# Strassen's method for the input product of a second MLP layer, one Trainium2 core

## Chip, core and metric

One NeuronCore of a Trainium2 chip runs the whole program. The metric is device time in microseconds (us) of one execution. Engines are called TensorE (PE, with its weight loads as PEld), VectorE (DVE), ScalarE (ACT), GpSimd (POOL) and SyncE (SP, which issues the DMAs).

## What is computed

Attention with rotary embedding, then two MLP layers (called moe and moe2 in the reference) on the same 1152 tokens, width 512, hidden width 2048. The change concerns the second layer:

```python
x = attention_with_rope(q, k, v)           # B=2, H=8, S=576, D=64 -> (1152, 512)
h = x @ w_in;   g = where(h > 0, h, exp(min(h, 0)) - 1);   x = g @ w_out      # layer 1
h = x @ w2_in;  g = h * tanh(log1p(exp(h)));               out = g @ w2_out   # layer 2
```

The four weight matrices arrive as 64-bit floats, the rest as 32-bit floats.

## The kernel before

**Precision.** Each fp32 operand of a product is held as a rounded half "h" and a remainder "l" (lo), and each product is made of three passes: h·h, h·l, l·h. For activations, `XH`/`XL` hold the layer's input (hidden on partitions in four chunks `cc` of 128, tokens along the row).

**Weights.** A block of weights (512 KB) lands in `raw` (three buffers), is turned from 64-bit to 32-bit in `wu` by one GpSimd multiplication (L96, "rebase") and three VectorE bit operations (L100, L104, L108), is rounded by ScalarE (L126), and GpSimd subtracts to get the lo half (L127). There are 16 input blocks and 16 output blocks per layer. A pair of feature blocks (2 x 128 hidden features) is the unit of the input product.

**Input product.** `g1_mm` (L180) makes one unit: one feature pair times one third of the tokens (384), in 24 matmuls of 384 columns, into a PSUM tile `ps_s`; that tag has two buffers, so a unit waits until the unit two before has been read. A layer has 8 pairs x 3 thirds = 24 units. Layer 1 follows with the ELU on ScalarE and VectorE, layer 2 with Mish on ScalarE (L772), rounding (L773) and a subtraction on VectorE (L774).

**Output product.** Layer 1 (`g2_first`, L783): 24 matmuls of 384 columns per tile of third x two output chunks, added into `Y`, and in the last group `XH` (L803) and `XL` (L804) of the next layer are made from it. Layer 2 (`g2_second`, L806): per group of four feature blocks and per 128 tokens 12 matmuls of 512 columns, added into `Y` by VectorE (L820), 36 tiles of them.

**Order.** In layer 1 every engine runs in the order in which the code is written. In layer 2 ScalarE alone does; for the other engines a scheduler chooses. On every engine an instruction that waits holds up all behind it. Layer 2's first units were placed among layer 1's last output tiles.

Of the kernel before, what the change touches and what calls it, by code (L numbers as in the profile page):

```python
# [18 lines left out]
MANUAL = {mybir.EngineType.Activation}  # L19
# [7 lines left out]
def kernel(  # L27
# [23 lines left out]
    GF = 4  # L51
# [18 lines left out]
    late_pool = [None]  # L70

# [14 lines left out]
    def weight_stages(key):  # L86
        kind, c = key
        raw = raws.pop(key)
        if wide:


            w = raw.rearrange("p (n w) -> p n w", w=2)
            low, high = w[:, :, 0], w[:, :, 1]
            u = wpool.tile([128, 512], F32, tag="wu", name="wu", bufs=2)
            ui = u.bitcast(I32)
            nc.gpsimd.tensor_scalar(  # L96
                out=u, in0=high.bitcast(F32), scalar1=REBASE, scalar2=0.0, op0=ALU.mult, op1=ALU.add
            )
            yield
# [3 lines left out]
            yield  # L103
# [3 lines left out]
            yield  # L107
# [3 lines left out]
            yield  # L111
        else:
            u = raw
        even = c // GF % 2 == 0
        tag, bufs = ("wi", "wo")[kind] + ("0" if even else "1"), GF
        if kind and even:
            bufs = GF // 2
            tag += "b" * (c % GF >= bufs)
        pool = wpool if even and tag[-1] != "b" else late_pool[0]
        hi = pool.tile([128, 512], F32R, tag=tag + "h", name=tag + "h", bufs=bufs)  # L120
        lo = pool.tile([128, 512], F32R, tag=tag + "l", name=tag + "l", bufs=bufs)
# [4 lines left out]
        nc.scalar.activation(out=hi, in_=u, func=AF.Copy)  # L126
        nc.gpsimd.tensor_tensor(out=lo, in0=u, in1=plain(hi), op=ALU.subtract)  # L127

    jobs = []
    for g in range(2 * NG):  # L130
        for kind in range(2):
            jobs += [(kind, g * GF + i) for i in range(GF)]
    loaded, opened, njob = [0], [0], [0]
# [21 lines left out]
    def weight_part(depth=2):  # L155
        while len(running) < depth and opened[0] < len(jobs):
            open_job()
        if running:
            advance(0)

    def weight_job():
        n = min(njob[0] + 1, len(jobs))
        while njob[0] < n:
            weight_part()
# [36 lines left out]
    def tmp(tag):  # L201
        return late_pool[0].tile([128, 2 * CH], F32, tag=tag, name=tag, bufs=4)
# [7 lines left out]
    def galloc(m, fp, t):  # L210
        i = g_count[0] % GB
        g_count[0] += 1
        pool, tag, bufs = (main, "ge", GE) if i < GE else (late_pool[0], "g", GB - GE)
# [552 lines left out]
    units = [(m, g * GF // 2 + k, t) for m in range(2) for g in range(NG) for t in range(NT // CH) for k in range(GF // 2)]  # L766

    def moe(mp, early):
        def mish(unit, o):
            s = tmp("ta")  # L770
            gh, gl = galloc(*unit)
            nc.scalar.activation(out=v2(s), in_=o[:, :, :CH], func=AF.Mish)  # L772
            nc.scalar.activation(out=gh, in_=s, func=AF.Copy)  # L773
            nc.vector.tensor_tensor(out=gl, in0=s, in1=plain(gh), op=ALU.subtract)  # L774

        Yt = []

        def get_y():
            if not Yt:
                Yt.append(mp.tile([128, NC * NT], F32, name="Y"))  # L780
            return Yt[0]

        def g2_first(g, t, ep):  # L783
            o = g_pool[0].tile([128, 2, 512], F32, tag="g", name="ps_g", bufs=2)
            k = 0
            for f in range(g * GF, g * GF + GF):
                for w, i in ((0, 0), (0, 1), (1, 0)):
# [6 lines left out]
                    k += 1  # L794
            pv = o[:, :, :CH]
            part = (slice(None), slice(2 * ep, 2 * ep + 2), slice(t * CH, t * CH + CH))
            y = get_y().rearrange("p (e s) -> p e s", e=NC)[part]
# [4 lines left out]
            if g == NG - 1:  # L802
                nc.scalar.activation(out=XH[part], in_=y, func=AF.Copy)  # L803
                nc.vector.tensor_tensor(out=XL[part], in0=y, in1=plain(XH[part]), op=ALU.subtract)  # L804

        def g2_second(g, t):  # L806
            o = g_pool[0].tile([128, 512], F32, tag="h", name="ps_h", bufs=2)
            c, s0 = divmod(t * 128, CH)
            k = 0
            for f in range(NF + g * GF, NF + g * GF + GF):  # L810
                gh, gl = (g_part(f, c, i)[:, s0:s0 + 128] for i in range(2))
                hi, lo = WO[f]
                for l, w in ((gh, hi), (gl, hi), (gh, lo)):
                    nc.tensor.matmul(o, lhsT=l, rhs=w, start=(k == 0), stop=(k == 3 * GF - 1))  # L814
                    k += 1
            y = get_y().rearrange("p (t e) -> p t e", e=DM)[:, t, :]
            if g == 0:
                nc.scalar.activation(out=y, in_=o, func=AF.Copy)
            else:
                nc.vector.tensor_tensor(out=y, in0=y, in1=o, op=ALU.add)  # L820
                if g == NG - 1:
                    nc.sync.dma_start(out=out[t * 128:t * 128 + 128, :], in_=y)

        half = len(units) // 2
# [3 lines left out]

        def run_g2(it):
            (g2_second if it[0] else g2_first)(*it[1:])  # L830

        def due(n):
            return 2 * GF + (n + 1) * 2 * GF // (UB * NT // CH)

        def count(n):
            if n < half - 1:
                return (0, 0, 2, 1, 2, 2)[n] if n < 6 else 1 + n % 2
            return max(0, min(len(jobs), due(n)) - njob[0])
# [157 lines left out]
```

## Time and profile before

| | |
|---|---|
| runs: median (lowest to highest) of 3 | 555.0 us (554.99 to 555.21) |
| the profiled execution's own time | 555.24 us |
| its span, first to last instruction | 553.4 us |
| TensorE busy | 544.7 us (98%) |
| VectorE, ScalarE, GpSimd busy | 369.1, 266.9, 246.7 us |
| granted TensorE clock | 1.000 of full speed |

The profiled time is 1.9 us more than the span, which is work around the first and last instruction. A share of busy time is a mean over stages: attention up to about 145 us, layer 1 up to about 360 us, layer 2 to the end. A busy TensorE counts pipelined matmuls, so what one matmul costs is read from the spacing of their starts and not from the duration of one.

### The profile page before, as it was taken

The page shows a single profiled execution, that of the slowest core. Times are in us where ns is not written, and L with a number is a line of the kernel's source. Part 1 is how long each engine was busy: PE and PEld are TensorE (multiplying, and loading weights), DVE is VectorE, ACT ScalarE, POOL GpSimd, SP SyncE. Part 2 cuts the span into 40 slices and gives each one's busy share as a digit, 9 for nine tenths or more (in the row PEclk, how much of TensorE's full clock was granted, in tenths as well). Part 3 has the DMA queues.
Part 4 walks back from the last instruction along what each step waited for, and adds up shares of the span by engine and source line. Part 5 has one row for each costly group of instructions (what it writes and reads, how often), then busy time and mean ns, then how long its engine had stood idle before and what let it go on. Part 6 is the DMA issues. An engine that isn't in the chain of part 4 may idle for free.

```text
span 553.4 us, 8762 instructions
## 1 busy us (share of the span) xinstructions
PE 544.7 (98%) x3306; PEld 498.2 (90%) x3306; DVE 369.1 (67%) x548; ACT 266.9 (48%) x462; POOL 246.7 (45%) x228
## 2 busy tenths in 40 slices
PE   8999999999999999999999999999999999999997
PEld 6678888887899999999999999999998989998985
DVE  4677776787977987988888978857436555521221
ACT  3666776677556666455445456254343133222120
POOL 6899988842424443453433431443424433220000
PEclk9999999999999999999999999999999999999999
DMA  8278888765422333232323221424323132000112
GB/s 250 93 195 220 210 215 229 175 160 129 127 77 78 114 115 114 77 114 76 114 79 111 80 76 42 151 76 132 94 81 114 39 115 61 16 0 1 38 39 96
DMA packets 49098, 59.78 MB, mean 108 GB/s; under 512 B 20768, under 2 KB 38944, under 8 KB 48288
## 3 DMA queue, kind: packets, MB, share of 16 engines
q1 hardware_dynamic: 48512, 58.64, 36.4%
q8 instruction: 26, 0.43, 0.3%
q10 hardware_dynamic: 544, 0.59, 0.3%
q14 instruction: 16, 0.13, 0.1%
HBM read 47.51 MB, written 2.36 MB: 90 GB/s over the span
## 4 chain that ended last, share of the span: by engine, by line
PE 86%; DVE 5%; ACT 3%; POOL 3%; DMA 2%; issue 1%; SPq 0%; ACTq 0%; POOLq 0%; DVEq 0%
PE ps_s L188 33%; PE ps_h L814 18%; PE ps_g L790 17%; PE ps_s L421 7%; PE psA L528 6%; PE psT L488 4%; DMA tab<-in_rope_dram 1%; DVE mn L428 1%; DVE wu L108 1%; ACT P L441 1%; DMA qb<-ql 1%; POOL qk_t L303 1%; POOL qk_t L300 1%; POOL qk_t L298 1%; DVE wu L104 0%
## 5 line engine op out<-in xcount | busy, mean ns | idle before, releaser
L428 DVE TENSOR_REDUCE mn<-ps_s 128x1 f32<-128x576 f32 x72 | 53.7, 755 | 25.2 <-PE ps_s L421 24.2
L772 ACT ACTIVATE ta<-ps_s 128x768 f32<-128x768 f32 x24 | 19.5, 812 | 100.8 <-PE ps_s L188 100.8
L100 DVE TENSOR_SCALAR wu<-wu 128x512 int32<-128x512 int32 x64 | 41.4, 647 | 38.6 <-POOL wu L96 38.6
L441 ACT ACTIVATE P<-ps_s,mn 128x576 f32<-128x576 f32 x72 | 52.9, 737 | 14.4 <-DVE mn L428 14.2
L104 DVE SCALAR_TENSOR_TENSOR wu<-raw,wu 128x512 int32<-128x512 int32 x64 | 51.0, 797 | 1.9
L188 PE MATMUL ps_s<-XH,wi0h 128*128 128x384 f32 x192 | 49.2, 337 | 0.1
L127 POOL TENSOR_TENSOR wi0l<-wu,wi0h 128x512 fp32r<-128x512 f32 x16 | 23.7, 1482 | 57.4 <-ACT wi0h L126 57.4
L108 DVE SCALAR_TENSOR_TENSOR wu<-raw,wu 128x512 int32<-128x512 int32 x64 | 47.8, 747 | 1.8
L127 POOL TENSOR_TENSOR wi1l<-wu,wi1h 128x512 fp32r<-128x512 f32 x16 | 24.2, 1521 | 55.5 <-ACT wi1h L126 55.5
L188 PE MATMUL ps_s<-XL,wi1h 128*128 128x384 f32 x192 | 48.9, 335 | 0.0
L188 PE MATMUL ps_s<-XL,wi0h 128*128 128x384 f32 x192 | 48.9, 335 | 0.0
L188 PE MATMUL ps_s<-XH,wi1l 128*128 128x384 f32 x192 | 48.8, 335 | 0.0
L188 PE MATMUL ps_s<-XH,wi0l 128*128 128x384 f32 x192 | 48.8, 335 | 0.0
L188 PE MATMUL ps_s<-XH,wi1h 128*128 128x384 f32 x192 | 48.7, 334 | 0.0
L96 POOL TENSOR_SCALAR wu<-raw 128x512 f32<-128x512 f32 x64 | 46.1, 726 | 3.9
L127 POOL TENSOR_TENSOR wo1l<-wu,wo1h 128x512 fp32r<-128x512 f32 x16 | 23.3, 1461 | 48.3 <-ACT wo1h L126 48.3
L488 PE MATMUL psT<-idn,P 128*128 128x128 f32 x288 | 43.0, 273 | 0.0
L774 DVE TENSOR_TENSOR g<-ta,g 128x768 fp32r<-128x768 f32 x16 | 17.5, 1093 | 37.0 <-ACT g L773 37.0
L528 PE MATMUL psA<-pt,v_t 128*64 128x256 f32 (+1 forms) x240 | 36.1, 401 | 0.6 <-ACT R L473 0.3
L508 ACT ACTIVATE pt<-psT 128x512 f32<-128x512 f32 x43 | 25.5, 594 | 22.6 <-PE psT L488 22.6
L488 PEld LDWEIGHTS psT<-idn,P 128*128 128x128 f32 x288 | 34.7, 141 | 1.9 <-issue 1.5
L188 PEld LDWEIGHTS ps_s<-XH,wi0h 128*128 128x128 f32 x192 | 34.5, 188 | 1.8 <-issue 0.8
(176 smaller groups left out, 1356.8 us busy)
## 6 DMA issues: line engine op xcount, KB each, us to landing
raw<-in_w_in_dram SPq DMA_DIRECT2D x32, 512.0 KB, 3.7
raw<-in_w_out_dram SPq DMA_DIRECT2D x32, 512.0 KB, 3.3
qk_t<-in_qk_dram SPq DMA_DIRECT2D x6, 1152.0 KB, 5.7
qa<-qh SPq DMA_DIRECT2D x24, 144.0 KB, 3.6
out_dram<-Y SPq DMA_DIRECT2D x9, 256.0 KB, 2.0
ka<-kh SPq DMA_DIRECT2D x12, 144.0 KB, 4.5
ka<-kl SPq DMA_DIRECT2D x12, 144.0 KB, 3.9
qb<-ql SPq DMA_DIRECT2D x12, 144.0 KB, 3.4
```

Source lines behind the costliest of these rows:

```text
L96: nc.gpsimd.tensor_scalar(out=u, in0=high.bitcast(F32), scalar1=REBASE, scalar2=0.0, op0=ALU.mult, op1=ALU.add)
L100: nc.vector.tensor_scalar(out=ui, in0=ui, scalar1=3, scalar2=0x7FFFFFF8, op0=ALU.logical_shift_left, op1=ALU.bitwise_and)
L104: nc.vector.scalar_tensor_tensor(out=ui, in0=high, scalar=-0x80000000, in1=ui, op0=ALU.bitwise_and, op1=ALU.bitwise_or)
L108: nc.vector.scalar_tensor_tensor(out=ui, in0=low, scalar=29, in1=ui, op0=ALU.logical_shift_right, op1=ALU.bitwise_or)
L127: nc.gpsimd.tensor_tensor(out=lo, in0=u, in1=plain(hi), op=ALU.subtract)
L188: nc.tensor.matmul(o[:, j, :CH], lhsT=ws[j][i][:, cc, :], rhs=x[:, cc, t * CH:t * CH + CH], start=(k == 0), stop=(k == 3 * NC - 1),)
L428: nc.vector.tensor_reduce(out=m, in_=psS[u][:, :, :HS], axis=AX.XY, op=ALU.min)
L441: nc.scalar.activation(out=P.rearrange("p (j n) -> p j n", j=2), in_=psS.pop(u)[:, :, :HS], func=AF.Exp, scale=-1.0, bias=mn_t.pop(u), acc ...
L488: nc.tensor.transpose(tv[:, c, :], P[:, k:k + 128], idn)
L528: nc.tensor.matmul(o[64 * h:64 * h + 64, cols], lhsT=v, rhs=rhs, start=(c == 0 and first), stop=(c == 4), skip_group_check=True,)
L790: nc.tensor.matmul(o[:, j, :CH], lhsT=WO[f][w][:, e * 128:e * 128 + 128], rhs=g_part(f, t, i), start=(k == 0), stop=(k == 3 * GF - 1),)
L814: nc.tensor.matmul(o, lhsT=l, rhs=w, start=(k == 0), stop=(k == 3 * GF - 1))
```

## The change

The second layer's input product is rebuilt. The token dimension is cut into two halves u (576 each, one per batch) and each half into two blocks of 288; the 512-wide contraction into top and low 256; a feature pair into its two blocks. For pairs 1 to 7 the 2 x 2 x 2 block product is made of 7 products (Winograd's form) and not 8. Pair 0 stays classic, three `g1_mm` units. The operands that Strassen needs are sums: four of weights per pair (`Pieces.sums`), and t1 to t4 of the activations, once per half (`form`, `put_hi`, `put_lo`). Sums of products are made partly in PSUM (three of the seven products are added into bank "a" on top of the first, one into bank "c"), with copies in between, and partly on VectorE. The output product runs per pair (6 matmuls of 512 columns, 72 tiles) and not per group (12 matmuls, 36 tiles). The rebase of layer 2's weights moves from GpSimd to ScalarE, but for pair 0's two input blocks. All engines' orders are those of the code.

```diff
-MANUAL = {mybir.EngineType.Activation}
...
+    def rebase(raw, tag, pool, on_act=False):
...
+        if on_act:
+            nc.scalar.activation(out=u, in_=high, func=AF.Copy, scale=REBASE)
...
+    class Pieces:
...
+        def sums(self):
+            w = self.w = late_pool[0].tile([128, 768], F32, tag="ws", name="ws", bufs=1)
+            s3, s2, s4 = (w[:, 256 * k:256 * k + 256] for k in range(3))
...
+            nc.vector.tensor_tensor(out=s3, in0=a11, in1=a21, op=ALU.subtract)
+            nc.vector.tensor_tensor(out=a21, in0=a21, in1=a22, op=ALU.add)
+            nc.vector.tensor_tensor(out=s2, in0=a21, in1=a11, op=ALU.subtract)
+            nc.vector.tensor_tensor(out=s4, in0=a12, in1=s2, op=ALU.subtract)
+
+        def round(self, k):
+            names = (("a11", "a12"), ("s1", "a22"), ("s3", "s2"), ("s4",))[k]
...
+            round_weight(hl[0][:, :n], hl[1][:, :n], src)
...
+        P = {
+            1: ("a11", "b11", "a"), 2: ("a12", "b21", "b"), 3: ("s4", "b22", "c"), 4: ("a22", "t4", "a"),
+            5: ("s1", "t1", "c"), 6: ("s2", "t2", "a"), 7: ("s3", "t3", "a"),
+        }
...
+            def mm(self, k):
...
+                for cc in range(NC // 2):
+                    for i, x in ((0, 0), (0, 1), (1, 0)):
+                        for u in range(2):
+                            nc.tensor.matmul(
+                                self.o[r][:, u, :H2], lhsT=w[i][:, cc, :], rhs=XO[u][xn][x][:, cc, :],
...
+            def copy(self, nm, r):
+                nc.scalar.activation(out=self.temp(nm), in_=self.bank(r), func=AF.Copy)
+
+            def add(self, nm, r):
+                x = self.temp(nm)
+                nc.vector.tensor_tensor(out=x, in0=x, in1=self.bank(r), op=ALU.add)
...
+            if pair.q == 0:
+                nc.scalar.activation(out=y, in_=o, func=AF.Copy)
+            else:
+                nc.vector.tensor_tensor(out=y, in0=y, in1=o, op=ALU.add)
...
+            x.classic(0)
+            w.sums()
+            w.round(0)
+            form(1, "t3")
+            put_hi(0, "t4")
+            put_hi(1, "t3")
...
+            w.round(1)
+            x.classic_act(0)
+            x.classic_hi(0)
...
+            for q in range(1, NQ):
...
+                x.mm(1)
...
+                x.copy("m1", "a")
...
+                x.mm(2)
+                x.add("m1", "b")
+                o[1].bits(1, 2)
+                x.mm(5)
+                x.act("m1")
+                x.copy("m5", "c")
+                x.lo("m1")
...
+                outs(2)
...
+                x.mm(6)
+                x.copy("u2", "a")
...
+                outs(2)
+                if more:
+                    w.sums()
+                x.mm(3)
+                x.add("u2", "c")
+                x.act("u2")
...
+                outs(2 if more else 1)
+                x.lo("u2")
+                x.mm(7)
+                x.copy("u3", "a")
...
+                x.add22()
+                outs(2 if more else 1)
+                x.act("u3")
+                x.mm(4)
+                x.lo("u3")
+                if more:
+                    o = [Block(NF + 2 * q + 2 + j) for j in range(2)]
+                    for b in o:
+                        b.load()
+                x.act("s")
+                outs(1 if more else 3)
+                x.lo("s")
+            queue.extend((x, t) for t in range(NT // 128))
+            outs(len(queue))
```

Three places in the engines' orders follow. The first is ScalarE where layer 2 begins. Before, the table load for Mish and the first Mish (out `ta`, from the unit's PSUM tile `ps_s`) stand directly behind the last ELU's work, with roundings of weights (`wo0bh`, `wi1h`) and of the layer's input (`XH`) in between:

```order
L772 ACT_TABLE_LOAD
L772 ACTIVATE ta<-ps_s 128x768
L126 ACTIVATE wo0bh<-wu 128x512
L773 ACTIVATE ge<-ta 128x768
L126 ACTIVATE wo0bh<-wu 128x512
L803 ACTIVATE XH<-Y 128x2x384
L126 ACTIVATE wi1h<-wu 128x512
L772 ACTIVATE ta<-ps_s 128x768
```

After, `xt_...` are the rounded t2, t3, t4, `wi1h<-wv` and `wi1h<-ws` the rounded weights of pair 1 and their sums; the three `ta<-ps_s` are the Mish of the three classic units:

```order
L905 ACTIVATE xt_3847<-gg 128x576
L116 ACTIVATE wi1h<-wv 128x512
L1093 ACT_TABLE_LOAD
L1093 ACTIVATE ta<-ps_s 128x768
L1096 ACTIVATE gg<-ta 128x2x384
L905 ACTIVATE xt_3885<-gg 128x576
L905 ACTIVATE xt_3887<-gg 128x576
L116 ACTIVATE wi1h<-ws 128x512
L116 ACTIVATE wi1h<-ws 128x256
L1093 ACTIVATE ta<-ps_s 128x768
L1096 ACTIVATE gg<-ta 128x2x384
L905 ACTIVATE XH<-gg 128x2x288
```

The table load and the first Mish now stand behind the rounding of the second half's t3 (`xt_3847`), which reads a VectorE result. Behind the last row shown come two rebases (`wu<-raw`) and then the third Mish.

The second place is VectorE at the same boundary. Before, from the last third's `Y` on, it has weight bits (`wu`) and little else:

```order
L801 TENSOR_TENSOR Y<-Y,ps_g 128x2x384
L804 TENSOR_TENSOR XL<-Y,XH 128x2x384
L244 TENSOR_TENSOR g<-tb,g 128x768
L100 TENSOR_SCALAR wu<-wu 128x512
L104 SCALAR_TENSOR_TENSOR wu<-raw,wu 128x512
L108 SCALAR_TENSOR_TENSOR wu<-raw,wu 128x512
```

After, `ta<-...` are t3, t2 and t4 of the first half, `ge` the lo halves of two of them, `ws`/`wv` the four weight sums, `gg<-Y` the second half's t3:

```order
L882 TENSOR_TENSOR ta<-Y 128x576
L882 TENSOR_TENSOR ta<-ta,Y 128x576
L882 TENSOR_TENSOR ta<-Y,ta 128x576
L932 TENSOR_TENSOR Y<-Y,ps_g 128x2x384
L909 TENSOR_TENSOR ge<-ta,ge 128x576 x2
L938 TENSOR_TENSOR XL<-Y,XH 128x2x384
L932 TENSOR_TENSOR Y<-Y,ps_g 128x2x384
L938 TENSOR_TENSOR XL<-Y,XH 128x2x384
L813 TENSOR_TENSOR ws<-wv 128x256
```

The second half's t3 stands four rows (the weight sums) behind the last row shown.

The third place is VectorE in the steady part of layer 2. Before, a piece from the middle of the layer:

```order
L820 TENSOR_TENSOR Y<-Y,ps_h 128x512
L100 TENSOR_SCALAR wu<-wu 128x512
L104 SCALAR_TENSOR_TENSOR wu<-raw,wu 128x512
L108 SCALAR_TENSOR_TENSOR wu<-raw,wu 128x512
L820 TENSOR_TENSOR Y<-Y,ps_h 128x512
L774 TENSOR_TENSOR g<-ta,g 128x768
```

After, from the middle of a pair, with `Y<-Y,ps_h` the output tiles, `ta<-ta,ps_s_4231` the addition of bank "c", `gg` the lo halves of results:

```order
L1115 TENSOR_TENSOR Y<-Y,ps_h 128x512 x2
L813 TENSOR_TENSOR ws<-wv 128x256
L814 TENSOR_TENSOR wv<-wv 128x256
L815 TENSOR_TENSOR ws<-wv 128x256
L816 TENSOR_TENSOR ws<-wv,ws 128x256
L1064 TENSOR_TENSOR ta<-ta,ps_s_4231 128x576
L1115 TENSOR_TENSOR Y<-Y,ps_h 128x512 x2
L1082 TENSOR_TENSOR gg<-ta,gg 128x2x288
L1068 TENSOR_TENSOR ta<-ta 128x576
L1115 TENSOR_TENSOR Y<-Y,ps_h 128x512 x2
L1082 TENSOR_TENSOR gg<-ta,gg 128x2x288
```

Sums, additions and twice as many `Y` rows are new between the weight bits.

## Rows read from the trace of the kernel before

**Rows 1.** The page: busy us, share of the span and instructions of each engine.
```profile
PE 544.7 (98%) x3306; PEld 498.2 (90%) x3306; DVE 369.1 (67%) x548; ACT 266.9 (48%) x462; POOL 246.7 (45%) x228
```

**Rows 2.** Busy time by stretch (us, instructions): PE, PEld, DVE, ACT, POOL; clock, DMA.
```profile
0.00:20.00 20.00, 16.74 (x98) 13.45 (x98) 10.82 (x28) 8.12 (x18) 15.67 (x24) 1.00 0.74 234
172.00:334.00 162.00, 162.00 (x936) 162.00 (x935) 138.65 (x165) 89.76 (x119) 67.50 (x60) 1.00 0.31 98
```

**Rows 3.** Chain that ended last: start us, us, engine, tile, line, matmuls.
```profile
333.84 4.16 PE ps_g L790 x24
...
367.12 5.48 PE ps_h L814 x24
372.61 4.18 PE ps_s L188 x24
...
533.26 16.38 PE ps_h L814 x72
549.66 0.69 DVE Y L820
```

**Rows 4.** Matmuls of 288 columns in attention, in order of time.
```profile
142.06 0.53 PE L421 MATMUL ps_s<-kh,bh 128*128 128x288 f32 x2
142.43 0.42 PE L421 MATMUL ps_s<-kl,bh 128*128 128x288 f32 x2
142.69 0.43 PE L421 MATMUL ps_s<-kh,bl 128*128 128x288 f32 x2
142.96 0.49 PE L488 MATMUL psT<-idn,P 128*128 128x128 f32 x3
```

**Rows 5.** Weight loads of the same matmuls, in order of time.
```profile
142.30 0.32 PEld L421 LDWEIGHTS ps_s<-kl,bh 128*128 128x128 f32 x2
142.56 0.32 PEld L421 LDWEIGHTS ps_s<-kh,bl 128*128 128x128 f32 x2
```

**Rows 6.** VectorE by tile: ns min/median/max, first to last start; 372 to 548 us.
```profile
L100 DVE TENSOR_SCALAR wu<-wu x20: 419/427/869, 372.2 to 481.1; 128x512 int32<-128x512 int32 x20
L104 DVE SCALAR_TENSOR_TENSOR wu<-raw,wu x20: 682/692/694, 373.1 to 481.6; 128x512 int32<-128x512 int32 x20
L108 DVE SCALAR_TENSOR_TENSOR wu<-raw,wu x20: 682/692/1670, 374.0 to 482.3; 128x512 int32<-128x512 int32 x20
L820 DVE TENSOR_TENSOR Y<-Y,ps_h x26: 674/687/689, 422.9 to 546.9; 128x512 f32<-128x512 f32 x26
L774 DVE TENSOR_TENSOR g<-ta,g x15: 951/957/2047, 374.6 to 535.0; 128x768 fp32r<-128x768 f32 x15
```

**Rows 7.** VectorE and GpSimd groups in 172 to 334 us: busy us, mean ns.
```profile
L104 DVE SCALAR_TENSOR_TENSOR wu<-raw,wu 128x512 int32<-128x512 int32 x30 | 27.2, 907 | 1.0
L100 DVE TENSOR_SCALAR wu<-wu 128x512 int32<-128x512 int32 x30 | 23.4, 781 | 0.0
L244 DVE TENSOR_TENSOR g<-tb,g 128x768 fp32r<-128x768 f32 x14 | 14.5, 1033 | 3.0 <-ACT g L240 2.7
```

**Rows 8.** GpSimd's subtraction, all of it for these blocks: busy us, mean ns.
```profile
L127 POOL TENSOR_TENSOR wo1l<-wu,wo1h 128x512 fp32r<-128x512 f32 x16 | 23.3, 1461 | 48.3 <-ACT wo1h L126 48.3
```

**Rows 9.** ScalarE groups: busy us, mean ns of one.
```profile
L772 ACT ACTIVATE ta<-ps_s 128x768 f32<-128x768 f32 x24 | 19.5, 812 | 100.8 <-PE ps_s L188 100.8
L818 ACT ACTIVATE Y<-ps_h 128x512 f32<-128x512 f32 x9 | 5.4, 596 | 11.0 <-PE ps_h L814 11.0
L126 ACT ACTIVATE wi1h<-wu 128x512 fp32r<-128x512 f32 x16 | 9.8, 624 | 8.6 <-DVE wu L108 8.6
L336 ACT ACTIVATE kh<-qk_t 128x576 fp32r<-128x576 f32 x1 | 0.7, 680 | 0.0
```

**Rows 10.** ScalarE and VectorE where layer 2 begins, in order of time.
```profile
340.92 1.28 ACT L772 ACT_TABLE_LOAD   x1
...
340.94 0.96 DVE L804 TENSOR_TENSOR XL<-Y,XH 128x768 fp32r<-128x768 f32 x1 [0.91 <-ACT XH L803]
```

**Rows 11.** DMA issues: KB each, median us to landing.
```profile
raw<-in_w_in_dram SPq DMA_DIRECT2D x32, 512.0 KB, 3.7
```

More of the change, by code (lines that the diff above doesn't have):

```diff
@@ L155, in weight_part @@
     def weight_part(depth=2):
[L156 removed]
+        while len(running) < depth and opened[0] < singles:
             open_job()
@@ L763, in attention @@
                 run_tail(u)
-    units = [(m, g * GF // 2 + k, t) for m in range(2) for g in range(NG) for t in range(NT // CH) for k in range(GF // 2)]
-    def moe(mp, early):
[L769 to L783, printed above, removed]
+    units = [(0, g * GF // 2 + k, t) for g in range(NG) for t in range(NT // CH) for k in range(GF // 2)]
@@ L803, in g2_first, with g2_xl @@
                 nc.scalar.activation(out=XH[part], in_=y, func=AF.Copy)
[L804 to L824, printed above, removed]
+        def g2_xl(t, ep):
+            part = (slice(None), slice(2 * ep, 2 * ep + 2), slice(t * CH, t * CH + CH))
+            nc.vector.tensor_tensor(out=XL[part], in0=Yf[part], in1=plain(XH[part]), op=ALU.subtract)
+        def g2_first(g, t, ep):
+            g2_y(g, t, ep, g2_mm(g, t, ep))
+            if g == NG - 1:
+                g2_xl(t, ep)
         UB = GF // 2
@@ new lines, in step @@
+            if n == 2:
+                advance(0)
+                advance(0)
+                todo = 0
+            if o is not None:
+                o = elu(units[n], o)
+                if n == 20:
+                    w.load(0)
+                elif n in (21, 22):
+                    first_out[n - 21].load()
+                o = elu_join(*o)
+            some(1)
+            if o is not None:
+                o = elu_hi(*o)
+            some(3)
+            if n == 20:
+                w.bits(0, 0, 1)
+            elif n in (21, 22):
+                first_out[n - 21].bits(0, 1, 2)
+            elif n == 23:
+                w.bits(1, 0, 1)
@@ L879, in step @@
+            if fp % UB == UB - 1:
+                pend.extend((n + 2, fp // UB, t, ep) for ep in range(NC // 2))
+            if pend and pend[0][0] <= n:
+                g2_first(*pend.pop(0)[1:])
+            if o is not None:
+                elu_lo(*o)
+            if n == 20:
+                w.bits(0, 2)
+                w.load(1)
+            elif n in (21, 22):
+                first_out[n - 21].round()
+            elif n == 23:
+                w.bits(1, 2)
             some(4)
-            if n >= half - 1:
-                for _ in range(count(n)):
-                    weight_job()
```

373 lines of the change are left out of this document (299 added, 74 removed).

## Prediction

> **What bounds the kernel now.** I read the shares first: TensorE is busy 98% of the span, VectorE 67% [rows 1]. A mean over stages says little, so next the stretches: from 172 to 334 us, layer 1, TensorE is busy 162.0 of 162.0 us, at clock 1.00 [rows 2]. Then the chain that ended last: from 333.84 on it is TensorE alone, without a gap, to the last 72 matmuls and one VectorE addition [rows 3]. So from there on time is won only by less TensorE work, and lost by whatever makes TensorE wait. What a matmul costs is read from that chain: 24 of 384 columns take 4.16 us (173 ns each), 24 of 512 take 5.48, 72 take 16.38 (228 ns each) [rows 3]. Both lie some 13 to 15 ns above columns at 2.4 GHz (160 and 213 ns).
>
> **What is removed on TensorE.** Up to the last but three output tiles of layer 1 TensorE's order is the old one, so I count from 333.84. Per pair, three units of 24 matmuls (4.18 us each between 512-column work [rows 3]) are 12.54 us. They become 7 products of 12 matmuls of 288 columns. Attention has such matmuls: starts at 142.43, 142.69 and 142.96 with two in each step [rows 4], 0.53 us for four, 132.5 ns each. That is again 120 ns plus 13. So 84 x 132.5 = 11.13 us, and some 20 ns for each of seven changes of width (4.18 against 4.16 [rows 3]): 11.27. Saved: 1.27 us a pair, 8.9 us in seven. The output product has 432 matmuls of 512 columns before and after. The bounds of the disputed price: 130 ns, and 185 ns, which is the first step behind another kind of matmul (142.06 to 142.43 for two [rows 4]); I take 132.5, since that step is paid once a change and not per matmul.
>
> **What is added at the boundary.** Here ScalarE and VectorE work in written order, and TensorE must wait for them. I walk it with durations of before; widths not seen are interpolated: VectorE 0.76 us for 576 columns and 0.42 for 256 (0.687 at 512, 0.957 at 768 [rows 6]), ScalarE 0.65 to 0.68 for 576 (0.60 at 512, 0.81 at 768, 0.68 seen [rows 9]).
>
> 1. TensorE does the last four output tiles of layer 1 in a row from 333.8, 4.16 us each, so to 350.5, then the classic units c0 and c1 to 358.8. c2 needs c0's PSUM buffer, so c0's Mish. VectorE before that: the first tile's `Y` stood at 339.1 and its `XL` at 340.94 [rows 10]; two bit operations are now ahead, so one us later; with the last ELU's lo, another bit operation and the second tile it gets to t3 at 347.1. Three forms (2.3), the third tile's `Y` (0.95), two lo halves (1.4) and its `XL` (0.9) bring it to 352.5; the fourth tile's `Y`, `XH` (ScalarE, 0.84), `XL` to 355.3; four weight sums (1.7) and the second half's t3 (0.76) to 357.7. ScalarE only now can round that t3 (0.68), round a weight (0.62), load the table (1.28 [rows 10]) and do c0's Mish (0.81): 361.1. Wait of c2: 2.4 us. Before, the same table load ran at 340.92, under other work [rows 10].
> 2. c2 ends at 365.2, pair 1's first product at 366.8; the second needs c2's buffer. Between Mish 0 and Mish 2 ScalarE has 0.85, 2 x 0.68, 0.62, 0.33, 0.81, 0.85, 0.68 and 2 x 0.62, so 6.7 us, then 0.8: 368.3. Wait: 1.5.
> 3. In pair 1 ScalarE, not VectorE, empties the nine output tiles (0.60 each [rows 9]). Output tile 3 needs tile 1's buffer; ScalarE comes to it behind m1 (which waits for VectorE's late addition, 373.6), m5, a rounding and a rebase, at 377.3; tile 3 was due at 375.9. Wait: 1.4.
> 4. With the rest of these copies ScalarE reaches the Mish of "s" at 392.0 and ends it at 392.7; pair 2's first product needs that buffer and was due at 391.7. Wait: 1.0.
>
> Sum of waits 6.3 us. Either bound: none of it, if ScalarE and VectorE run ahead of my walk by 2.4 us; 9 us, if one or two VectorE operations more are hit by GpSimd (next).
>
> **What is added in the steady pairs.** TensorE needs 11.1 + 54 x 0.228 = 23.4 us a pair. VectorE: bits 4 x (0.427 + 0.692 + 0.692) = 7.2 [rows 6], sums 4 x 0.42 = 1.7, three additions 2.3, four lo halves 3.0, nine `Y` 6.2 (0.687 each; 4.5 a pair before): 20.4 us without disturbance. GpSimd's subtractions disturb: from 172 to 334 us the mean of the first bit operation is 781 ns against 427, the lo's 1033 against 957 [rows 6, 7]. Over 30 subtractions that is (30 x 0.354 + 14 x 0.076) / 30 = 0.39 us each. A pair has 5.5 of them (3.5 for pieces and sums, 2 for outputs): 2.1, so 22.5 us, 0.9 below TensorE. ScalarE has 13.9 us a pair. The rebases on it (0.62 each by the nearest row [rows 9]) cost nothing while these stay below 23.4; the second piece's block is free for its DMA only some 4 us ahead of its rebase, against 3.7 to landing [rows 11], and a late one has 2 us until TensorE would see it. The tightest place is the end of the pair: addition of "c" on VectorE, two Mish, two rebases, then the Mish of "s", about 0.5 us ahead of the next pair's first product. I take no steady wait; up to 0.5 us a pair (3 us) goes into the range. The end of the program stays: 54 output matmuls, one `Y`, the store.
>
> **Sum.** 555.24 - 8.9 + 6.3 = 552.6 us for an execution like the profiled one, which lay 0.24 above the median; so 552.4 as a median.
>
> **Rivals.**
> - *VectorE becomes the bound in pairs 2 to 6: slower.* If each subtraction held VectorE up for all of its 1.46 us [rows 8], a pair would be 20.4 + 5.5 x 1.46 = 28.4, 5.0 over TensorE, 25 us in five pairs: 577. It decides from about 0.7 us per subtraction on (24.2 a pair, 3.9 us in five, more than the 2.6 gained and 0.2% besides). For it: single operations of 1670 and 2047 ns [rows 6], the 907 ns of the second bit operation [rows 7]; against it: 0.39 on average where VectorE was busy 139 of 162 us [rows 2], and medians that stay at the floor. The Trainium skill (SBUF — State Buffer, Who interferes with whom) says that a VectorE instruction with two SBUF inputs and a GpSimd one that reads SBUF exclude each other for the whole instruction; by that the time would go to 577, and the trace shows part of it. A partial form, 24 to 25 us a pair, gives 555 to 560. Together 21%.
> - *The boundary costs next to nothing: 546 to 549.* If VectorE overlaps more than I count, the table load and Mish come before 358.8 and the later waits shrink with the first. Against it: c0's Mish stands behind seven rows that all need the fourth tile, done only at 350.5. 13%.
> - *The 288-column matmul is bound by its weight load.* A load lasts 0.19 us; if the loads could not overlap the work before them, 588 x (188 - 132.5) ns = 33 us more: 585. Against it: second loads start 0.13 us behind the first (0.32 for two of 0.19 [rows 5]). 4%. The Trainium skill (TensorE: Matmul & The Clock Gate, Part 3: Packing small matmuls) says that a load overlaps running matmuls only in other row groups, which would price both kernels by load plus stream and leave no gain; these rows, with full-height loads, do not agree.
> - *The clock falls in the 2.4 us gap before c2.* At half the clock c2 takes 4.2 us more: 556.6. The clock was 1.00 even in the first 20 us, where TensorE idled 3.3 us in all [rows 2]. 5%.
>
> **How the numbers follow.** The likeliest case, gain less boundary waits, 57%, has 550 to 555 as its own range. The other cases are above. Two in ten may lie outside: 548 to 558 leaves out the far VectorE case, the loads and the best boundary. Within 0.2% (1.1 us, about what a measurement of this kernel can tell from no change) is 553.9 to 556.1. Faster: 46 of the 57 and the 13: 0.59. Same: 11 of the 57 and a part of the first rival: 0.17. Slower: the rest, 0.24.
>
> **What would show it.** TensorE's starts in a run of 12: 132 ns, and 1.6 us a product. Four waits: before c2 (2.4, for ScalarE's Mish behind a table load near 359), before pair 1's second product, before its third output tile, before pair 2. From pair 2 to 7 a period of 23.4 us with VectorE busy 21 to 23 of it. The prediction is wrong if the period is over 24, if the clock is below 1.00 behind the gap, or if TensorE waits at places not named.

## The result and the profile after

The changed kernel takes 560.73 us (median of 4 runs, 560.18 to 561.29) against 555.11: ratio 1.0100, 95% interval 1.0083 to 1.0118. It is slower by 1.0%, and outside the predicted range. Its profiled execution has a span of 558.4 us, 5.0 more than before. One of the four executions of the kernel with the later rebase, below, ran at a granted clock of 0.75 throughout and took 659 us; the median of the other three is 550.98 us, where all four give the 551.26 stated there. The page's busy times of the changed kernel, to be held against [rows 1]:

```profile
PE 538.0 (96%) x3390; PEld 488.5 (87%) x3390; DVE 443.5 (79%) x656; ACT 314.7 (56%) x556; POOL 239.2 (43%) x212
```

TensorE is busy 6.7 us less and idle 11.7 us more (20.4 against 8.7 us of the span). These are its waits from 330 us on (engine, tile and line, what it waited for; us in total, times, the longest):

```profile
PE ps_h L1109 <- DVE Y L1115: 5.0, 5, 1.6
PE ps_s L207 <- ACT ta L1093: 3.1, 1, 3.1
PE ps_h L1109 <- ACT Y L1113: 2.0, 2, 1.1
PE ps_h L1109 <- DVE gg L1082: 0.5, 1, 0.5
```

The second line is the forecast wait of c2 for c0's Mish, the third stands before pair 1's third and seventh output tiles. The first one was not forecast: five waits, one in each of pairs 2 to 6, before the third output tile. The fourth is at the end, where the low half of "s" comes behind three output additions. Next, stretches of the same trace (us; busy PE, PEld, DVE, ACT, POOL; granted clock; DMA), the last one inside the steady pairs:

```profile
358.00:362.00 4.00, 0.87 (x5) 0.58 (x4) 3.93 (x5) 3.90 (x5) 1.39 (x1) 1.00 0.00 0
362.00:366.00 4.00, 4.00 (x17) 4.00 (x16) 3.72 (x4) 3.97 (x8) 2.01 (x2) 0.60 0.00 0
366.00:372.00 6.00, 6.00 (x44) 6.00 (x43) 5.93 (x9) 4.71 (x8) 0.94 (x1) 0.98 0.00 0
420.00:470.00 50.00, 48.29 (x282) 43.04 (x281) 44.76 (x66) 26.44 (x44) 15.67 (x12) 1.00 0.27 85
```

Behind the gap the granted clock falls to a mean of 0.60 over 4 us, most of them at the lower of its two levels (1.2 and 2.4 GHz), and c2 is paid there. The chain that ended last, around c2 and through one steady pair (start, us, what), shows both losses, where [rows 3] had TensorE alone:

```profile
359.26 1.28 ACT L1093
360.56 0.82 ACT ta L1093
361.42 6.06 PE ps_s L207 x24
...
443.82 0.44 DVE Y L1115
...
447.97 1.65 DVE wu L107
...
451.38 1.67 DVE wv L107
453.05 0.61 DVE Y L1115
...
453.70 3.06 PE ps_h L1109 x12
456.76 1.60 PE ps_s L1040 x12
...
468.58 0.49 DVE Y L1115
```

c2's 24 matmuls take 6.06 us instead of 4.16. In the pair, VectorE's bit operations lead the chain up to the third tile. From one "Y" to its like in the next pair is 24.76 us; before, a pair took 12.54 + 54 x 0.228 = 24.9. TensorE's own work, seven products of 1.58 us and the same 54 output matmuls, is 23.4. So the pairs in the middle win 0.1 us each where 1.5 was there to be won.

Added up from the starts of TensorE's matmuls, over the usual distance of two starts: c2 5.0 us (3.13 wait, 1.9 clock), pair 1's output tiles 2.5, pair 2 2.1, pairs 3 to 6 1.35 each, the end 0.8. That is 15.8 us. Seven pairs give back 7 x 1.5 = 10.4. The difference, 5.4, is the loss of span (5.0) to within half a microsecond.

What makes VectorE late is seen beside GpSimd. First VectorE, then GpSimd, in order of time in that pair (the first row is the first of ten operations that stand ahead of the output additions at 452.97; five of the ten are shown):

```profile
445.09 0.42 DVE L103 TENSOR_SCALAR wu<-wu 128x512 int32<-128x512 int32 x1
...
447.22 0.75 DVE L1064 TENSOR_TENSOR ta<-ta,ps_s 128x576 f32<-128x576 f32 x1
447.88 1.73 DVE L107 SCALAR_TENSOR_TENSOR wu<-raw,wu 128x512 int32<-128x512 int32 x1
449.64 0.69 DVE L111 SCALAR_TENSOR_TENSOR wu<-raw,wu 128x512 int32<-128x512 int32 x1
...
451.38 1.67 DVE L107 SCALAR_TENSOR_TENSOR wv<-raw,wv 128x512 int32<-128x512 int32 x1
452.97 1.27 DVE L1115 TENSOR_TENSOR Y<-Y,ps_h 128x512 f32<-128x512 f32 x2
...
455.94 1.66 DVE L111 SCALAR_TENSOR_TENSOR wv<-raw,wv 128x512 int32<-128x512 int32 x1
```

```profile
447.77 1.29 POOL L117 TENSOR_TENSOR wo0l<-wu,wo0h 128x512 fp32r<-128x512 f32 x1 [5.53 <-ACT wo0h L116]
451.13 1.36 POOL L117 TENSOR_TENSOR wo0l<-wu,wo0h 128x512 fp32r<-128x512 f32 x1 [2.08 <-issue]
455.66 1.40 POOL L117 TENSOR_TENSOR wi1l<-wv,wi1h 128x512 fp32r<-128x512 f32 x1 [3.16 <-ACT wi1h L116]
```

Three bit operations of 0.69 us take 1.66 to 1.73, and each ends 0.54 to 0.56 us after the GpSimd subtraction that ran beside it (449.06 and 449.61, 452.49 and 453.05, 457.06 and 457.60). Those that meet none take 0.69. Such a lengthening is called a hold-up below.

### The profile page after: what moved, and what is told of

Read it like the earlier page. It is cut to its first block, busy times and chain, and to the rows that moved or that the text cites. A ratio compares the mean times of both kernels' runs of the same rounds, so it can differ in the third digit from the quotient of the medians.

```text
span 558.4 us, 9091 instructions
## 1 busy us (share of the span) xinstructions
PE 538.0 (96%) x3390; PEld 488.5 (87%) x3390; DVE 443.5 (79%) x656; ACT 314.7 (56%) x556; POOL 239.2 (43%) x212
## 4 chain that ended last, share of the span: by engine, by line
PE 74%; DVE 15%; ACT 3%; issue 3%; POOL 3%; DMA 1%; ACTq 0%; SPq 0%; DVEq 0%; POOLq 0%
PE ps_s L207 19%; PE ps_g L918 16%; PE ps_h L1109 14%; PE ps_s L441 7%; PE ps_s L1040 6%; PE psA L548 6%; PE psT L508 4%; DVE wu L107 3%; DVE wv L107 2%; DVE gg L1082 1%; DVE Y L1115 1%; DMA tab<-in_rope_dram 1%; DVE ta L1064 1%; DVE wu L111 1%; DVE mn L448 1%
## 5 line engine op out<-in xcount | busy, mean ns | idle before, releaser
L1115 DVE TENSOR_TENSOR Y<-Y,ps_h 128x512 f32<-128x512 f32 x63 | 41.2, 680 | 16.3 <-PE ps_h L1109 16.3
L1109 PE MATMUL ps_h<-wo0bh,gg 128*128 128x512 f32 x144 | 45.5, 396 | 3.8 <-DVE Y L1115 3.3
L1109 PE MATMUL ps_h<-wo0h,gg 128*128 128x512 f32 x144 | 45.3, 396 | 3.7 <-ACT Y L1113 2.0
L117 POOL TENSOR_TENSOR wo0l<-wu,wo0h 128x512 fp32r<-128x512 f32 x12 | 17.7, 1477 | 58.8 <-ACT wo0h L116 52.6
L254 DVE SCALAR_TENSOR_TENSOR tb<-ta,tb 128x768 f32<-128x768 f32 x22 | 21.4, 975 | 19.9 <-ACT tb L250 19.8
L1109 PEld LDWEIGHTS ps_h<-wo0bh,gg 128*128 128x128 f32 x144 | 26.1, 188 | 10.1 <-DVE Y L1115 4.1
L207 PE MATMUL ps_s<-XH,wi0h 128*128 128x384 f32 x120 | 31.5, 344 | 3.1 <-ACT ta L1093 3.1
L1109 PEld LDWEIGHTS ps_h<-wo0h,gg 128*128 128x128 f32 x144 | 25.8, 188 | 9.3 <-ACT Y L1113 2.4
L207 PE MATMUL ps_s<-XL,wi0h 128*128 128x384 f32 x120 | 31.2, 341 | 0.0
L207 PE MATMUL ps_s<-XH,wi0l 128*128 128x384 f32 x120 | 31.2, 341 | 0.0
```

The lines of the kernel that those rows point to most:

```text
L207: nc.tensor.matmul(o[:, j, :CH], lhsT=ws[j][i][:, cc, :], rhs=x[:, cc, t * CH:t * CH + CH], start=(k == 0), stop=(k == 3 * NC - 1),)
```

## The experiments

The theory after this reading has three parts. The steady waits come from VectorE operations held up by GpSimd in the first half of the pair, not from the amount of VectorE's work; the boundary's waits come from the order on ScalarE and VectorE; and the fall of the clock comes from the gap. The rival is that VectorE has too much to do, so that any order only shifts the waits.

**Mish of c0 early.**

```diff
             w.round(0)
+            x.classic_act(0)
+            x.classic_hi(0)
             form(1, "t3")
...
             w.round(1)
-            x.classic_act(0)
-            x.classic_hi(0)
             put_lo(1, "t3")
```

> The Mish and the rounding of the first classic unit are written ahead of the second half's t3, so that ScalarE does the table load near 355 us and the Mish by 357.5. Theory (the boundary wait and the lower clock behind it cost 3.1 and 1.9 us): the unit c2 starts without a wait at about 358.6, the clock stays 1.00, and the time falls by about 5 us, to 555.7. Rival (the work is only shifted: a wait of the same size comes up later in the boundary, since VectorE is what is late): the wait before c2 goes, but pair 1's first output tile or pair 2 starts hardly earlier, and the time stays over 559.

560.2 us, ratio 1.0086 [1.0062, 1.0111]. c2 waits no more; the wait and the fall of the clock stand one step later, before pair 1's second product, as the wait and a stretch behind it show:

```profile
PE ps_s L1040 <- ACT ta L1093: 3.8, 1, 3.8
```

```profile
366.00:372.00 6.00, 4.24 (x17) 4.24 (x18) 5.93 (x10) 4.12 (x7) 0.00 (x0) 0.52 0.00 0
```

The rival's outcome: a wait moved, not removed.

**Spare matmuls in the gap** (13 of 512 columns, whose result nobody reads).

```diff
             put_lo(1, "t2")
+            spare = g_pool[0].tile([128, 512], F32, tag="h", name="ps_h", bufs=2)
+            wk = WI[NF][0]
+            for i in range(13):
+                nc.tensor.matmul(
+                    spare, lhsT=wk[:, 0, :], rhs=wk.rearrange("p c f -> p (c f)"), start=(i == 0), stop=(i == 12)
+                )
             x.classic(2)
```

> Thirteen matmuls of 512 columns (about 3.0 us) into a PSUM tile that is not read are put between the classic units c1 and c2, where TensorE otherwise waits 3.1 us. Theory (the fall of the clock is caused by that gap): the granted clock stays 1.00 there, c2 takes 4.2 us instead of 6.1, and the time falls by 1 to 2 us, to about 559. Rival (the clock falls for something else, such as the hours before): clock below 1.00 all the same, and no gain.

560.65 us, 1.0102 [1.0074, 1.0131]. The stretch that had 0.60:

```profile
362.00:366.00 4.00, 4.00 (x23) 4.00 (x24) 3.75 (x5) 3.97 (x7) 1.47 (x1) 1.00 0.00 0
```

c2 takes 4.29 us: the gap did bring the clock down. The time stays all the same, a miss against the 1 to 2 us expected, since pair 1's products and tiles now wait 0.8, 1.5 and 1.0 us: behind c2 TensorE has to wait for ScalarE and VectorE, which are no further than before.

**GpSimd without reading** (from pair 1 on it sets the low halves of the weights to zero, so the kernel leaves out the pass that uses them).

```diff
-        nc.gpsimd.tensor_tensor(out=lo, in0=u, in1=plain(hi), op=ALU.subtract)
+        if no_lo[0]:
+            nc.gpsimd.memset(plain(lo), 0.0)
+        else:
+            nc.gpsimd.tensor_tensor(out=lo, in0=u, in1=plain(hi), op=ALU.subtract)
...
             for q in range(1, NQ):
                 prev, x = x, Pair(q)
+                no_lo[0] = True
```

> From pair 1 on GpSimd writes zeros as the lo halves of the weights (memset) in place of the subtraction, so this kernel leaves the third pass's weight part out; the number of GpSimd's instructions and all other work stay. Theory (VectorE's bit operations of 1.65 to 1.72 us are held up by GpSimd's subtraction, which reads SBUF, and this makes the output tiles wait): the bit operations go back to 0.69 us, the wait before the third output tile goes, the period of a pair falls from 24.8 to about 23.5 us, and the time by 6 to 8 us, to about 553. Rival (VectorE's queue is too long in the first half of a pair even without GpSimd, or the hold-up is from anything GpSimd does): the period stays over 24.3.

552.95 us, 0.9961 [0.9941, 0.9981]. Some two steady pairs:

```profile
420.00:470.00 50.00, 50.00 (x295) 45.10 (x294) 42.07 (x70) 28.16 (x46) 5.42 (x12) 1.00 0.27 86
```

TensorE is full, a pair takes 23.6 us, and of the third-tile wait some 0.2 us are left. c2's wait is as it was (3.1 us). Since the memsets also ran at other times, and VectorE was busy 19.7 us a pair instead of 22.2, this alone doesn't part "reads" or "at that moment" from "amount".

**First two output tiles ahead of the next pair's bits.**

```diff
                     w.load(1)
-                    w.bits(0, 0, 1)
                 outs(2)
                 if more:
-                    w.bits(0, 2)
+                    w.bits(0, 0, 1, 2)
```

> In each pair the first two additions into Y stand ahead of the next pair's first two bit operations on VectorE, not behind them; nothing else is moved. Theory (the third output tile waits 0.85 to 1.1 us a pair because these additions stand behind held-up bit operations): that wait goes, the period falls by about 1 us in pairs 2 to 6, and the time by 4 to 5 us, to about 556. Rival (VectorE as a whole is the bound of a pair): the wait comes back at the fifth or seventh tile, the period stays within 0.3 us of 24.8.

557.55 us, 1.0040 [1.0023, 1.0057]. This lies between the two expectations. Two long operations are left instead of three (1.73 and 1.67 us), the third-tile wait falls from 0.85 to 0.39, a pair takes 24.1, and VectorE is busy 21.45 us of it.

**Another order at the boundary** (each Mish first, t1 ahead of t3 and t4, in pair 1 the output copies ahead; a part of it):

```diff
             w.round(0)
+            x.classic_act(0)
+            x.classic_hi(0)
+            form(0, "t1")
+            form(1, "t1")
-            form(1, "t3")
             put_hi(0, "t4")
...
+            x.classic_act(1)
+            x.classic_hi(1)
+            put_hi(0, "t1")
             put_hi(1, "t2")
```

> Only the order at the boundary and in pair 1 is changed, no work is left out: ScalarE does each classic unit's Mish first thing after that unit, VectorE forms and rounds t1 before t3 and t4 of the second half, whose lo halves come last, and in pair 1 the copies of output tiles on ScalarE stand ahead of the work that waits for VectorE. Theory (the boundary's waits come from what stands ahead of a Mish or a copy, not from the amount of VectorE's work): no wait before c2, none before pair 1's second and fifth product above 0.5 us, clock 1.00, pair 1 without waits; 5.0 + 2.4 us less, about 553.5. Rival (the amount of VectorE's work between the last tile of layer 1 and pair 1 is what is too long, so each reordering only moves the wait): the waits up to the start of pair 2 still sum to 5 us or more and the time stays over 557.

560.94 us, 1.0107 [1.0093, 1.0121]. No gain. Its waits:

```profile
PE ps_h L1109 <- DVE Y L1115: 5.0, 5, 1.6
PE ps_h L1109 <- ACT Y L1113: 2.7, 1, 2.7
PE ps_s L1040 <- DVE XL L909: 1.7, 2, 0.9
```

c2's wait is gone; t1's low halves and a copy behind u2's Mish are late instead, and the clock has 0.83 from 366 to 372. This spoke for the rival.

**Both output blocks rounded together, behind m1** (on the kernel with two output tiles ahead of the bits; besides, the low half of "s" ahead of the last output tiles).

```diff
-                o[0].round()
                 x.mm(2)
...
                 x.lo("m1")
+                o[0].round()
                 o[1].round()
```

> Only the order inside the pairs is changed: the first two additions into Y ahead of the next pair's bits, the rounding of the first output block behind the lo half of m1, so that GpSimd's first subtraction runs beside the additions into Y, and in the last pair the lo half of s ahead of the last additions. Theory (the wait comes from additions into Y that stand behind bit operations held up by GpSimd, not from the sum of VectorE's work): no wait before the third output tile, period 23.6 us or less, no wait before the last nine tiles; 1.1 x 5 + 1.7 + 0.9 us less, about 553. Rival (VectorE's sum with hold-ups, 22 to 23 us, is the bound): period stays at 24.2 or more as with the additions alone moved.

559.28 us, 1.0074 [1.0061, 1.0088]: worse than the 557.55 without it. A pair takes 24.85 us (23.9 in one of them), which is what the rival expected. The waits at the end and before the third tile are gone, and one of 1.1 us stands before the fifth tile. The two subtractions run as one block of 2.56 us, past the output additions into the next bit operation:

```profile
427.20 0.69 DVE L1115 TENSOR_TENSOR Y<-Y,ps_h 128x512 f32<-128x512 f32 x1 [0.51 <-PE ps_h L1109]
427.81 1.52 DVE L103 TENSOR_SCALAR wv<-wv 128x512 int32<-128x512 int32 x1
```

```profile
426.48 2.56 POOL L117 TENSOR_TENSOR wo0bl<-wu,wo0bh 128x512 fp32r<-128x512 f32 x2 [8.33 <-ACT wo0bh L116]
```

The addition, which reads PSUM, keeps its 0.69; the bit operation with a single input in SBUF, 0.42 elsewhere, takes 1.52. This run also tells amount from order: in a pair of 24.85 us VectorE is busy 21.5 us, no more than in the kernel that it is built on, whose pair takes 24.1.

**The last two orders together.**

> The last two kernels' changes together. Theory (both losses are of order and add up): about 15 us less than the changed kernel, 545 to 547, some 1.5% faster than the kernel before. Rival (a better boundary is given back inside the pairs, or the other way round): over 550.

559.24 us, 1.0077 [1.0063, 1.0091], as the rival had it: the waits of both kernels, one beside the other (1.7 for t1's low halves, 3.9 for a copy, 4.8 for "Y").

**The same subtractions, late.** The two output tiles ahead of the bits are part of this edit too, so what the place of the subtractions is worth is read against that kernel's 557.55 us.

```diff
-                o[0].round()
                 x.mm(2)
...
                 x.lo("m1")
-                o[1].round()
+                o[0].round()
                 if more:
                     w.load(1)
-                    w.bits(0, 0, 1)
                 outs(2)
                 if more:
-                    w.bits(0, 2)
+                    w.bits(0, 0, 1, 2)
...
-                    w.bits(1, 0, 1)
-                    w.round(0)
-                    w.bits(1, 2)
+                    w.bits(1, 0, 1, 2)
...
                 x.act("u2")
+                o[1].round()
                 if more:
+                    w.round(0)
                     w.round(1)
-                    w.round(2)
...
                 if more:
+                    w.round(2)
                     w.round(3)
```

> Edit: the same GpSimd subtractions at other times in every pair. The first output block is rounded when VectorE has done the low half of m1 (beside two output additions, which read PSUM), the second one and the pieces a11/a12 and s1/a22 only behind u2's Mish, s3/s2 and s4 behind the copy of u3; the next pair's bit operations stand together behind the first two output tiles. VectorE's and GpSimd's work stays the same in kind and count. Theory (a GpSimd subtraction holds up a VectorE operation that lies wholly in SBUF for as long as it runs; in the pair's first half these hold-ups add up to the wait at the third output tile): no bit operation of pairs 3 to 6 takes over 0.8 us, the 0.85 us wait is gone, a pair takes 23.6 to 23.9 us instead of 24.8, and the time is 554 to 555.5. Rival (only the amount counts, wherever the subtractions stand; or the later rounding makes weights late): the hold-ups turn up on other operations and a wait of the same size with them, a pair takes 24.4 us or more, and the time is 558 or above. The boundary keeps its 3.1 us wait and its fall of the clock.

553.24 us, 0.9967 [0.9956, 0.9978]: 7.5 us below the changed kernel, 4.3 below the one with only the output tiles moved. A pair takes 23.7 us, and TensorE has no wait left in pairs 2 to 6. VectorE's groups in pairs 2 to 6 of the changed kernel (busy us, mean ns):

```profile
L107 DVE SCALAR_TENSOR_TENSOR wu<-raw,wu 128x512 int32<-128x512 int32 x10 | 12.1, 1208 | 0.2
L107 DVE SCALAR_TENSOR_TENSOR wv<-raw,wv 128x512 int32<-128x512 int32 x10 | 11.8, 1180 | 0.3
L1068 DVE TENSOR_TENSOR ta<-ta 128x576 f32<-128x576 f32 x5 | 4.8, 957 | 4.1 <-ACT ta L1060 4.1
```

and of this one:

```profile
L1068 DVE TENSOR_TENSOR ta<-ta 128x576 f32<-128x576 f32 x5 | 8.4, 1686 | 6.7 <-ACT ta L1060 6.7
L107 DVE SCALAR_TENSOR_TENSOR wv<-raw,wv 128x512 int32<-128x512 int32 x10 | 6.9, 693 | 0.3
L107 DVE SCALAR_TENSOR_TENSOR wu<-raw,wu 128x512 int32<-128x512 int32 x10 | 6.9, 689 | 0.2
L103 DVE TENSOR_SCALAR wv<-wv 128x512 int32<-128x512 int32 x10 | 6.7, 671 | 0.0
```

Hold-ups have gone over to u3's addition in the second half, where VectorE has time. One expectation was missed: the bit operation of the last row, 0.42 us before, is still held up once a pair, to 0.86 us or more.

VectorE's operations are the same in kind and count, but its busy time is not: 22.2 us of 24.8 in a pair of the changed kernel, 21.1 of 23.7 here, since less of GpSimd's time now meets operations that it holds up. So this run alone does not part place from amount. The runs together do. With 21.45 and 21.5 us of VectorE a pair took 24.1 and 24.85 us in the two kernels that differ in order; with 21.1 and 19.7 us it took the same 23.6 to 23.7, here and without GpSimd's reads. The busy time does not set the length of the pair, and for the steady pairs the rival falls.

**Boundary and pair 1 by due time** (on the last kernel; in pair 1 the sum into u2 ahead of the bits and sums for pair 2, t1's low halves ahead of the tiles'; a part of it).

```diff
+            x.mm(3)
+            x.add("u2", "c")
+            outs(2)
+            x.act("u2")
+            o[1].round()
+            w.bits(0, 0, 1, 2)
+            x.lo("u2")
...
+            x.add22()
+            w.bits(1, 0, 1, 2)
```

> Edit: as the run with late subtractions, with the boundary and pair 1 written by due time as well: each classic tile's Mish ahead on ScalarE, t1's low halves ahead of the classic tiles' low halves, and in pair 1 the sum into u2 ahead of the bit operations and block sums for pair 2; the low half of s before the last three output tiles in the last pair. Theory (the boundary's 7.4 us over the matmuls' own time and pair 2's 1.7 come from the order in which VectorE, busy without a break from 354 to 384 us, does things that are due early and late): TensorE waits under 3 us in all between 350 and 420 us, the granted clock stays at 0.97 or above in every stretch, and the time is 547 to 551, below the kernel before's 555. Rival (VectorE's amount in these 30 us is the bound, whatever its order, as the other boundary order suggested, which moved the waits from c2 to pair 1's products and tiles): waits of 5 us or more remain there, the clock falls once, and the time is 552.5 or above, within 1.5 us of the run with late subtractions.

553.67 us, 0.9973 [0.9959, 0.9987]: no better than the kernel that it is built on. The signs are the rival's: from 350 to 420 us TensorE waits 4.9 us (5 or more were expected), the clock falls once, and the time stays. The trace gives another cause for the largest of these waits. ScalarE stands at a rebase for its DMA, with two output copies behind it, and VectorE later waits for the Mish of u2 behind them:

```profile
376.75 0.66 ACT L92 ACTIVATE wv<-raw 128x512 f32<-128x512 f32 x1 [3.09 <-DMA raw<-in_w_in_dram]
377.31 0.64 ACT L1060 ACTIVATE ta<-ps_s 128x576 f32<-128x576 f32 x1
377.85 1.08 ACT L1113 ACTIVATE Y<-ps_h 128x512 f32<-128x512 f32 x2
...
385.02 0.76 DVE L1082 TENSOR_TENSOR gg<-ta,gg 128x576 fp32r<-128x576 f32 x1 [4.50 <-ACT gg L1079]
```

TensorE waits 2.2 us for these copies, behind which the clock falls (0.70 from 378 to 382 us), and VectorE, far from full, stands idle 4.50 us before the low half of u2.

**That rebase later** (with two smaller moves: bit operations earlier, one rounding behind the Mish of "s").

```diff
             o[0].round()
-            w.load(1)
             x.mm(6)
...
             o[1].bits(0, 1, 2)
+            w.bits(0, 0, 1, 2)
             x.mm(3)
...
             x.act("u2")
+            w.load(1)
             o[1].round()
-            w.bits(0, 0, 1, 2)
             x.lo("u2")
+            w.bits(1, 0, 1, 2)
```

> Edit: the order by due time with three moves in pair 1. The rebase of pair 2's second raw block, on which ScalarE stood 3.09 us for its DMA at 376.75, ahead of the output copies, goes behind u2's Mish; the bit operations of the first block before the sum into u2 and those of the second before the copy of u3; the rounding of s1/a22, on which ScalarE stood 1.42 us ahead of the Mish of s, behind that Mish. Theory (what is left of the boundary's waits is two in-order queues with a waiting instruction at their head, not VectorE's amount): the waits on the output copies (2.24 us) and on the temporary of s (1.17 us) go, with them the 1.64 us of clock, about 5 us together, and the time is 548 to 550.5. Rival (VectorE has too much to do in these 30 us): waits of 2 us or more return at the next products or in pair 2, and the time stays at 552 or above.

551.26 us, 0.9935 [0.9918, 0.9951], the fastest of all: 3.6 us below the kernel before, 9.5 below the changed one, and between the two expectations. The waits are read from a single execution of the same kernel at the full clock:

> The kernel of the run with the later load once more, for a profile at the full clock: that run's profiled execution had a granted clock of 0.75 from its first to its last stretch, which hides every wait. Theory (two in-order queues with a waiting instruction at their head were what was left): TensorE waits under 2 us in all after 350 us, no stretch between 350 and 420 us has a clock below 0.97, time about 551. Rival (VectorE's amount): waits of 3 us or more are there, at pair 1's products or in pair 2.

551.14 us. Waits and two stretches:

```profile
PE ps_h L1109 <- DVE Y L1115: 1.9, 3, 1.0
PE ps_s L1040 <- ACT sx L1078: 1.5, 1, 1.5
PE ps_s L1040 <- POOL wi0l L117: 0.6, 1, 0.6
```

```profile
362.00:372.00 10.00, 10.00 (x66) 9.44 (x65) 9.31 (x13) 8.84 (x17) 3.36 (x2) 1.00 0.00 0
372.00:386.00 14.00, 14.00 (x78) 12.32 (x77) 11.70 (x15) 8.44 (x16) 4.96 (x3) 1.00 0.38 118
386.00:410.00 24.00, 20.35 (x116) 17.61 (x115) 20.95 (x33) 13.07 (x24) 6.28 (x5) 1.00 0.34 108
```

From c0 to the last tile of pair 1 TensorE has no gap at all and the clock stays at 1.00. But 4 us of waits stand in pair 2, to which part of VectorE's and ScalarE's work has moved, and that is the sign that was written down for the rival. Added up by TensorE's starts from c0 to the end of pair 2, the loss is 5.1 us here, 6.6 with the late subtractions alone and 9.7 in the changed kernel. So this order is worth 1.5 us at the boundary; for the remainder the cause stays open. VectorE isn't full there (20.95 of 24 us in the last row), and in pair 2 two bit operations in a row, ahead of the output additions, are held up by GpSimd, which points to place again but was not tested:

```profile
391.05 1.74 DVE L107 SCALAR_TENSOR_TENSOR wu<-raw,wu 128x512 int32<-128x512 int32 x1
392.82 1.67 DVE L111 SCALAR_TENSOR_TENSOR wu<-raw,wu 128x512 int32<-128x512 int32 x1
```

**No reads at the boundary** (on the late subtractions; pair 1's four weight tiles get zero low halves, which leaves out the pass that uses them).

> Edit: the run with late subtractions, in which GpSimd only sets the low halves of pair 1's four weight tiles to zero at the boundary (this leaves out the low pass of pair 1's weights); the order stays. Theory (three of the boundary's hold-ups, 1.09, 1.08 and 1.58 us, are VectorE operations behind GpSimd's reads, and the first of them stands ahead of the sums that ScalarE waits for before the first Mish): VectorE's first block difference takes 0.42 instead of 1.51 us, c2's wait falls from 3.14 to about 2.0 us, its slow clock remains, and the time is 551 to 552.5. Rival (the hold-ups at the boundary cost nothing, since the Mish waits for something else): c2's wait stays at 3.1 us and the time at 553.2.

551.56 us, 0.9943 [0.9926, 0.9959]. The first block difference takes 0.42 instead of 1.51 us and c2's wait falls to 2.05, as the theory had it; the time falls by 1.7 us, to the expected 551 to 552.5. A miss in the same run: the clock stays at 1.00 behind this shorter gap, where it was expected to fall.

## Why the prediction was wrong

- **The price of TensorE's work** held: 1.58 us a product, 132 ns each. By it the saving was 1.5 us a pair, not 1.27, since the changes of width cost next to nothing; the shortest pairs of any run, 23.6 us, had 1.3 of it. Weight loads did not bound it.
- **"I take no steady wait"** is the step that failed: 7.5 us in pairs 2 to 6, more than the 5.6 that the change lost. It compared a pair's sum of VectorE time (22.5 us) with TensorE's (23.4) and allowed a mean hold-up of 0.39 us per subtraction.
  - The mean was too small by the prediction's own rows: the second bit operation, 907 ns against 692 [rows 6, 7], was left out. With it the mean is 0.60 us and the sum 23.7. Pairs 3 to 6 had 0.57 us (3.4 us on six subtractions).
  - The sum still came out near the forecast, 22.2 us. That is luck, since the undisturbed work was smaller than counted (18.7 us, by difference, and not 20.4).
  - The wrong step is to take the sum for the condition. With 22.2 us VectorE was idle for 2.6 us of each pair, and TensorE waited all the same. VectorE works in order, and ten operations of 0.42 to 1.73 us, from 445.09 to 452.97, stood ahead of the addition that frees the third output tile's buffer, two of them held up by 1.0 us each. Nor is a hold-up a mean: it is up to 1.0 us where an operation with all its operands in SBUF starts early in a subtraction, less where it starts late, and nothing where an addition from PSUM runs beside it. The two orders with the same VectorE time (24.1 and 24.85 us a pair) show it, and the late subtractions with no wait left.
  - The rival "VectorE becomes the bound" named the engine and, with its partial form of 24 to 25 us a pair, the size; its reason, the amount, was not the cause.
- **Wait of c2** (2.4 us): the wait was right in place and cause, 3.1 in size; the 0.7 more is within the 1.09 that GpSimd's first subtraction cost ahead of the Mish. To it came 1.9 us of clock, which a rival held at 5% and priced at 4.2: the clock of 1.00 in the first 20 us, for which I put it so low, was another case, with no gap over 1.5 us.
- **Pair 1's second product** (1.5) and **pair 2's first product** (1.0): no wait in either place. **Third tile of pair 1** (1.4): there, with the like wait before the seventh tile 2.5 in all. One such wait can take another's place, as the early Mish, the spare matmuls and the first boundary order showed, each leaving the time where it was.
- **The end stays**: it cost 0.8 us, the low half of "s" behind three additions; moved ahead, its wait was gone.

In sum 15.8 us of waits and clock against the 6.3 forecast.

## What to carry over

An engine that works in order is not judged by its sum over a period: add up what stands ahead of each instruction that another engine waits for, with hold-ups at full length, and look for a waiting instruction at a queue's head (here a rebase for its DMA). A wait that vanishes without moving the time has gone somewhere: look one step later in the trace before giving the order up. The place of a second engine's work can matter though that engine is far from full: moving GpSimd's six subtractions a pair was worth 4.3 us here, with GpSimd busy 7.8 us of a pair's 24.8.

## What the runs showed of the hardware

In these traces a VectorE operation that lies wholly in SBUF and starts while a GpSimd subtraction (both inputs in SBUF) runs ends only behind that subtraction: with two inputs of 512 columns 0.55 us behind it (0.69 us alone, up to 1.73), with one input 0.28 behind it (0.42 alone, up to 1.52). Additions with an operand in PSUM ran beside it at 0.69. The Trainium skill (SBUF — State Buffer, Who interferes with whom) states the exclusion for two SBUF inputs against a reading GpSimd, and for the two-port forms of operations with one, in each case for the whole instruction. The rows agree with the first; they agree with the second if the bit operation with one input has such a form, which no row shows. It does not follow that every subtraction costs its length: in the changed kernel three in a pair met such an operation at nearly their full length, three did not.

The granted clock fell to a mean of 0.60 over 4 us behind a gap of 3.1 us, and to 0.70 behind one of 2.2 in another kernel, but not behind one of 2.05 in a third; two gaps under a microsecond each in 366 to 372 us went with 0.83 in a fourth. The traces don't settle which pattern counts.
